# exp(k) times v by one matmul of 64 columns a head, the constant inside the queries' sum, and moved ranks in an attention and two-layer kernel

## The chip, the cores and the metric

One core of one Trainium2 chip. The metric is the device time of one execution in microseconds (us). TensorE is called PE (its weight loads PEld), VectorE DVE, ScalarE ACT, GpSimd POOL, SyncE SP. SP issues the DMAs.

## What is computed

```
k_s  = exp(k - max_s k);  k_s /= sum_s k_s + 1e-9          # per batch, head, column; q alike, along its last axis
kv   = einsum('bhsd,bhse->bhde', k_s, v)                   # 8 batches, 8 heads, 576 rows, 64 columns
x    = einsum('bhsd,bhde->bhse', q_s, kv)  -> (4608, 512)
x    = relu(x @ w_in)**2 @ w_out                           # 512 -> 2048 -> 512
out  = (sigmoid(x @ w_gate) * (x @ w_val)) @ w_out2        # 512 -> 1536 -> 512
```

The inputs of the matrices are 64-bit floats and are turned into 32-bit words on the chip.

## The kernel before

**Blocks.** The 4608 rows are nine blocks `j` of 512. Two heads stand side by side in 128 columns, so there are four pairs `p`. For each batch `b` and pair `p` (32 calls) the keys go through `k_max` (maxima on DVE, lines 430 and 434), `k_turn` and `k_all` (transpose and spreading on PE, lines 440 and 452), `k_sub` (DVE, line 457), `k_exp` (ACT, line 461), `k_mm` (PE, line 467), `k_rec` (DVE) and `k_copy` (ACT, line 479). In `k_mm`, five float32 matmuls, one for each 128 rows of the sequence, contract exp(k) of both heads (128 columns, stationary) with v of both heads and a column of ones (129 columns, moving). Of the 128x128 result only the two diagonal 64x64 blocks are used; the column at 128 holds the sums. The ones come with v from the input: its rows are 130 wide, 128 of v, a one (zero in the padding rows) and a zero.

**Queries.** For each block and pair: maxima (`q_red`), `q_sub`, `q_exp`, sums (`q_red`), `q_sum`, `q_mul`, a transpose, and `q_mm` with the batch's kv (line 577). For blocks from 2 on a row of 64 columns is split over two partition groups, and `q_swap` (PE, line 524, 16 moving columns) brings the other half's sum, which `q_both` adds; `q_sum` then adds 1e-9 and takes the reciprocal.

**The two layers.** Each large product is made of three matmuls on rounded high and low parts (`mm3`, lines 217 to 219). Blocks 0 to 2 pass `w_in` and `w_out` one by one (`conv_in`, `conv_out`); the other blocks go in pairs through seven products of 2x2 blocks. Weights are loaded raw (`plan_raw`, tile `wraw`, lines 254 to 284), split (`plan_split`, `whl`), combined (`plan_sums`, line 298), stored to DRAM and fetched again when used (`plan_fetch`, `ws`). `plan_first` and `plan_late` prepare the first layer's weights, `plan_w` those of the second (nine calls).

**Order.** Nothing is issued in the order of the loops. Every step is given to a planner by `add(rank, {engine: us}, name, function, ..., after, take, give)`. `Plan.trace` runs a list schedule on the host: for each engine it takes, among the steps whose predecessors are done in its own reckoning, the one of lowest rank, and issues it; `take` and `give` count buffers. So ranks and the assumed durations (and `LATENCY` and `slack`) set only the order in which each engine's queue is filled, SP's too; on the chip each queue runs in that order and waits by semaphores. Ranks are built from stage starts: `T0` (block 0 passes `w_in`), `T2`, `T3`, `T4`, `T1`, with the steps `TS0`, `TS1`, `TS2` of a slice of 128 columns of the first layer. `plan_k` and `plan_q` rank the steps of keys and queries at `key + n * step`; `plan_blocks` places blocks 1 to 8.

Of the kernel before, what the change touches and what calls it, by code (L numbers as in the profile page):

```python
# [29 lines left out]
class Plan:  # L30
# [3 lines left out]

    LATENCY = {DMA: 3.0, PE: 0.2, DVE: 0.13, ACT: 0.15}
    LOOK = 48
# [106 lines left out]
def attention_mlp_mlp(  # L143
# [178 lines left out]
    def plan_split(kind, g, i, b, t, ts, after, give=(), htag="W"):  # L322
        key = (kind, g, i)
        add(t, {ACT: AS}, ("wh",) + key, w_hi, key, b, htag, after=after, take=[htag])
        add(t + 0.2, LOW, ("wo",) + key, w_lo, key, b, CHOSEN, after=[("wh",) + key], give=give)
        add(ts, {DMA: 1.5}, ("ws",) + key, w_store, key, after=[("wo",) + key], slack=STORE, give=[] if htag == "X" else ["W"])

# [34 lines left out]
    def plan_first(kind, g, times, tag):  # L362

        ready, own = {}, {}
        for b in range(4) if kind == "in" else (0, 2, 1, 3):
            t = times[b]
            done = plan_raw(kind, g, b, t - 8, tag, 8.0)
            i = SPLIT[b]
            plan_split(kind, g, i, b, t - 5, t - 4, done, htag="X")
            end = [("wo", kind, g, i)]  # L370
            if kind == "in":
                add(t - 3.9, {DMA: 0.8}, ("w32", kind, g, b), w_store32, (kind, g, b), after=done)
                end.append(("w32", kind, g, b))
# [16 lines left out]
    def plan_w(kind, g, T, dT, tag):  # L390

        ready = {b: plan_raw(kind, g, b, T + b * dT, tag, 6.0) for b in range(4)}
        t = T + 4 * dT
# [25 lines left out]
    def v_load(b, p):  # L419
        vt = tile4("W", "vt", F32, (128, RK, 2 * D + 2)) if b == 0 else tile2("v", "vt", (128, RK, 2 * D + 2))  # L420
        nc.sync.dma_start(out=vt, in_=v[b, p])
        vt_t[b, p] = vt

    def k_max(b, p, r):
# [38 lines left out]
    def k_mm(b, p):  # L463
        kt, vt = kt_t.pop((b, p)), vt_t.pop((b, p))
        ps = kps[b, p]
        for r in range(RK):
            nc.tensor.matmul(ps[:, 0:2 * D + 1], kt[:, r, :], vt[:, r, 0:2 * D + 1], start=(r == 0), stop=(r == RK - 1))  # L467

    def k_rec(b, p):
        ri = sp.tile([128, 1], F32, tag="kri", name="kri")  # L470
        nc.vector.tensor_scalar(out=ri, in0=kps[b, p][:, 2 * D:2 * D + 1], scalar1=1e-9, scalar2=None, op0=ALU.add)
        nc.vector.reciprocal(out=ri, in_=ri)
        kmx[b, p] = ri

    def k_copy(b, p):
        ps, ri = kps.pop((b, p)), kmx.pop((b, p))
        for h in range(2):
            s = slice(D * h, D * h + D)
            nc.scalar.activation(out=kvf[b % 2][p][s, s], in_=ps[s, s], func=AF.Copy, scale=ri[s])

# [64 lines left out]
    def q_sum(j, p):  # L545
        sm, s2 = q_both(j, p, ALU.add)
        nc.vector.tensor_scalar(out=s2, in0=s2, scalar1=1e-9, scalar2=None, op0=ALU.add)
        nc.vector.reciprocal(out=s2, in_=s2)
# [48 lines left out]
    kv_users = defaultdict(list)  # L597
    SLACK = 2.5
    slack = lambda j: SLACK if j > 4 else 0.0

    def plan_k(b, p, key, step, wait=()):
# [20 lines left out]
    def plan_q(j, p, key, step):  # L622
# [9 lines left out]
        if not pe:  # L632
            add(key + 2.3 * step, {PE: 0.15}, ("qbw",) + n, q_swap, j, p, after=[("qb",) + n], take=["pa"], slack=slack(j))
        add(key + 2.5 * step, {DVE: 0.36 if pe else 0.55}, ("qr",) + n, q_sum, j, p, after=[("qb" if pe else "qbw",) + n], give=[] if pe else ["pa"])
        add(key + 3 * step, {DVE: TT}, ("qm",) + n, q_mul, j, p, after=[("qr",) + n], give=["qr"])
# [286 lines left out]
    T1 = T4 + TS2 * F1 + 4  # L922
# [8 lines left out]
    for g in range(NU):  # L931
        plan_late("in", g, T3 + 10 + 35 * g, 4.0, "w")

    kvs = [("kv", 0, p) for p in range(NP)]

    def conv_fetch(j, kind, g, ii, t):

        if j:
            for i in ii:
                plan_fetch((kind, g, i), c_use(j, kind, g, i), t - 14)  # L940

    def conv_in(j, f, t):
# [6 lines left out]
        for kt in range(KT):  # L949
# [11 lines left out]
            if f % 2 and kt % 2:  # L961
                add(t, {FREE: 0.0}, ("cf", j, f, kt), lambda: None, after=[("ch", j, f, kt)] + ([] if j else [("ws", "in", g, i)]), give=[tag])
        add(t + 2.6, {ACT: 1.17}, ("cg", j, f), c_g, j, f, after=[("ch", j, f, KT - 1)], take=["f"])

    def conv_out(j, f, t):
# [5 lines left out]
        if f % 2 == 0:  # L971
            conv_fetch(j, "out", g, ii, t)
        add(t - 2.5, {ACT: AS}, ("chi", j, f), c_hi, j, f, after=[("cg", j, f)], take=["S"])
        add(t - 2, LOW, ("clo", j, f), c_lo, j, f, CHOSEN, after=[("chi", j, f)], give=["f"])
# [61 lines left out]
    def plan_in(uid, t, kind, g, xn, n, tags, last_unit, slow):  # L1036
# [3 lines left out]
        def pe(i, pr, t, wait):  # L1040
            use = (uid, i)
            plan_fetch((kind, g, i), use, t - 14)
            names = []
# [21 lines left out]
    def out_seven(n, h, js, G, t):  # L1065
# [6 lines left out]
        def pe(i, pr, t, wait):  # L1072
            for kk in range(4):
                if kk % 2 == 0:
                    plan_fetch(("out", 2 * h + kk // 2, i), (uid, i, kk // 2), t - 14)
                nm = ("p", uid, i, kk)
# [8 lines left out]
        def load(nm, b, t):  # L1085
            k_ = key(nm, b)
            add(t - 14, {DMA: 0.8}, ("old",) + k_, o_ld7, k_, (uid, nm, b), after=[("ost",) + k_ + (0,), ("p", ("u1", n, 1, 1), 3, 1)], take=["a"])
            return ("old",) + k_
# [16 lines left out]
    def in_stage(n, t):  # L1105
# [3 lines left out]
        mm = MM if len(js) > 1 else MH  # L1109
        plan_x(("X1", n), js, t - 22, ("x",), nt)  # L1110
        for h in range(2):
            G = ("G", n, h)
            gready = defaultdict(dict)
            for u in range(2):
# [4 lines left out]
                for b in range(2):  # L1119
                    for nm in ("s1", "s5", "s2"):  # L1120
                        add(t - 1, {ACT: 1.17, DVE: TT}, E(nm + "g", b), e_relu2, uid, nm, b, CHOSEN, after=[end[nm][b]])
                    add(t + 0.2, {ACT: 1.17}, E("p4g", b), e_relu2p, uid, "p4", prs[0], b, nt, "f", after=[end["p4"][b]], take=["f"])
# [4 lines left out]
            for kk in range(4):  # L1127
# [4 lines left out]
                for qn, (name, where) in gready[kk].items():  # L1132
# [5 lines left out]
                    ready[qn] = [("gbind", nm, qn)]  # L1138
                times = {i: t + 24 * mm * SLOW * x + 6 * mm * kk - 6 for x, i in enumerate(PRODUCTS)}
                plan_b(nm, ready, times, "S", nt, {qn: ["f"] for qn in ready})  # L1140
# [59 lines left out]
    def gate_stage(n, t):  # L1200
# [26 lines left out]
        for kk in range(gv_n):  # L1227
# [49 lines left out]
    for stage, n in STAGES:  # L1277
# [3 lines left out]
        else:  # L1281
            x_before["gate", n] = before
            before = [("xl", "x2", j, kt) for j in GATE[n] for kt in range(KT)]
    plan_blocks([1], T0 + 6, TS0 * F1 - 20)
    plan_blocks([2], T2 + 6, TS1 * F1 - 30)
    plan_blocks(IN[0], T3 + 5, (T1 - T3 - 40) / 2)

    BESIDE = {0: 1, 1: 2}
    t = T1
    for i, (stage, n) in enumerate(STAGES):  # L1290
        if i in BESIDE:
            js = IN[BESIDE[i]]
            plan_blocks(js, t + 4, ((D1 if stage is in_stage else D2_) - 60) / len(js))
# [76 lines left out]
```

## Time and profile before

| | before |
|---|---|
| median of 3 runs | 1667.49 us (1666.01 to 1671.13) |
| the profiled execution | 1665.63 us, its span 1663.9 us |
| mean granted clock of TensorE | 0.998 |
| PE busy | 1625.4 us (98%) |
| DVE busy | 1224.7 us (74%) |
| ACT busy | 939.1 us (56%) |
| DMA | 470.50 MB, mean 283 GB/s |

The busy times are of one execution, which the hardware profiler recorded; the span goes from its first to its last instruction. Matmuls are pipelined: one is still running when the next starts, so the mean of one is longer than its share of PE's time. A float32 matmul stands in the trace as two passes, each with a weight load of its own.

### The profile page before, as it was taken

How to read it: one execution, taken by the hardware profiler on the slowest of the kernel's cores; microseconds unless marked ns; L12 is line 12 of the kernel's file. 1: busy time of each engine (PE TensorE's matmuls, PEld its weight loads, DVE VectorE, ACT ScalarE, POOL GpSimd, SP SyncE). 2: the span in 40 equal slices, each digit the busy share in tenths (PEclk: the TensorE clock that was granted, in tenths of full speed). 3: DMA queues.
4: the chain of work that ended last, by engine and by line, in shares of the span. 5: the costliest groups of instructions: out<-in, count | busy, mean ns of one | idle time of the engine just before them, and what ended most of it. 6: DMA issues, size and time to landing. Idle time of an engine off the chain costs nothing.

```text
span 1663.9 us, 24397 instructions
## 1 busy us (share of the span) xinstructions
PE 1625.4 (98%) x8644; PEld 1391.4 (84%) x8644; DVE 1224.7 (74%) x2307; ACT 939.1 (56%) x1672; POOL 2.0 (0%) x14
## 2 busy tenths in 40 slices
PE   6899999999999999999999999999999999999998
PEld 4687788877888878888878889888988899889998
DVE  8999946779999999999797486347724683448446
ACT  5876745558686776777774354335533453335344
POOL 0000000000000000000000000000000000000000
PEclk9999999999999999999999999999999999999999
DMA  7999998799799979898989667766676667665896
GB/s 278 335 365 327 346 367 333 276 333 396 268 343 327 352 261 338 287 370 317 346 329 372 232 201 233 230 196 209 223 231 195 194 204 240 197 194 178 262 376 248
DMA packets 156633, 470.50 MB, mean 283 GB/s; under 512 B 16480, under 2 KB 25696, under 8 KB 156512
## 3 DMA queue, kind: packets, MB, share of 16 engines
q1 hardware_dynamic: 156512, 468.94, 80.7%
q8 instruction: 69, 1.13, 0.3%
q14 instruction: 52, 0.43, 0.1%
HBM read 372.93 MB, written 95.94 MB: 282 GB/s over the span
## 4 chain that ended last, share of the span: by engine, by line
PE 88%; DVE 6%; ACT 3%; DMA 2%; issue 1%; SPq 0%; DVEq 0%; ACTq 0%
PE bank L217 28%; PE bank L219 28%; PE bank L218 28%; PE kps L467 2%; PE xps L577 2%; DVE bS L214 1%; DMA ws<-w_in 1%; DMA qt<-in_q_dram 1%; DVE bX L214 1%; DVE whl L214 0%; DVE xp L733 0%; PE qsw L524 0%; DVE s L671 0%; DVE wf L284 0%; DMA w_gv<-whl 0%
## 5 line engine op out<-in xcount | busy, mean ns | idle before, releaser
L217 PE MATMUL bank<-bX,ws 128*128 128x512 f32 (+1 forms) x1176 | 445.0, 378 | 2.6 <-DMA ws<-w_in 2.5
L218 PE MATMUL bank<-bX,ws 128*128 128x512 f32 (+1 forms) x1176 | 440.2, 374 | 0.0
L219 PE MATMUL bank<-bX,ws 128*128 128x512 f32 (+1 forms) x1176 | 440.1, 374 | 0.0
L733 DVE TENSOR_TENSOR s<-s,bank 128x512 f32<-128x512 f32 (+1 forms) x297 | 191.4, 654 | 216.2 <-PE bank L219 177.6
L211 ACT ACTIVATE s<-bank 128x512 f32<-128x512 f32 (+1 forms) x297 | 168.4, 572 | 213.5 <-PE bank L219 210.3
L211 ACT ACTIVATE bS<-s 128x512 fp32r<-128x512 f32 (+1 forms) x330 | 194.8, 601 | 132.0 <-PE bank L219 112.5
L214 DVE TENSOR_TENSOR bS<-s,bS 128x512 fp32r<-128x512 f32 (+1 forms) x330 | 214.5, 656 | 62.6 <-ACT bS L211 62.1
L217 PEld LDWEIGHTS bank<-bX,ws 128*128 128x128 f32 x1176 | 221.6, 188 | 42.7 <-DMA ws<-w_in 3.3
L219 PEld LDWEIGHTS bank<-bX,ws 128*128 128x128 f32 x1176 | 221.4, 188 | 40.0
L218 PEld LDWEIGHTS bank<-bX,ws 128*128 128x128 f32 x1176 | 221.7, 189 | 37.8 <-issue 0.5
L217 PE MATMUL bank<-ws,bS 128*128 128x256 f32 x756 | 214.0, 283 | 0.0
L218 PE MATMUL bank<-ws,bS 128*128 128x256 f32 x756 | 213.9, 283 | 0.0
L219 PE MATMUL bank<-ws,bS 128*128 128x256 f32 x756 | 213.9, 283 | 0.0
L752 ACT ACTIVATE s<-s 128x512 f32<-128x512 f32 (+1 forms) x120 | 70.8, 591 | 154.2 <-DVE s L733 153.9
L217 PEld LDWEIGHTS bank<-ws,bS 128*128 128x128 f32 x756 | 145.0, 192 | 1.2 <-ACT s L211 0.4
L218 PEld LDWEIGHTS bank<-ws,bS 128*128 128x128 f32 x756 | 145.1, 192 | 0.7
L219 PEld LDWEIGHTS bank<-ws,bS 128*128 128x128 f32 x756 | 145.1, 192 | 0.0
L217 PE MATMUL bank<-bS,ws 128*128 128x512 f32 x336 | 134.2, 400 | 1.3 <-issue 0.4
L218 PE MATMUL bank<-bS,ws 128*128 128x512 f32 x336 | 131.4, 391 | 1.9 <-DVE bS L214 1.9
L219 PE MATMUL bank<-bS,ws 128*128 128x512 f32 x336 | 131.1, 390 | 0.0
L671 DVE TENSOR_TENSOR s<-s,s 128x512 f32<-128x512 f32 (+1 forms) x192 | 122.2, 655 | 1.7 <-ACT s L739 0.2
L211 ACT ACTIVATE whl<-wf 128x512 fp32r<-128x512 f32 x127 | 78.8, 628 | 38.5 <-DVE wf L284 20.4
(115 smaller groups left out, 2408.1 us busy)
## 6 DMA issues: line engine op xcount, KB each, us to landing
ws<-w_out SPq DMA_DIRECT2D x221, 512.0 KB, 4.9
ws<-w_gv SPq DMA_DIRECT2D x210, 512.0 KB, 4.3
ws<-w_in SPq DMA_DIRECT2D x116, 512.0 KB, 6.4
w_out<-whl SPq DMA_DIRECT2D x53, 512.0 KB, 5.2
w_gv<-whl SPq DMA_DIRECT2D x42, 512.0 KB, 5.2
w_in<-whl SPq DMA_DIRECT2D x32, 512.0 KB, 4.8
wraw<-in_moe_w_out_dram SPq DMA_DIRECT2D x28, 512.0 KB, 6.8
vt<-in_v_dram SPq DMA_DIRECT2D x32, 325.0 KB, 6.4
```

Of the source, the lines that this page charges most:

```text
L211: nc.scalar.activation(out=dst, in_=src, func=AF.Copy)
L214: by_name[engine].tensor_tensor(out=dst, in0=src, in1=hi.bitcast(F32), op=ALU.subtract)
L217: nc.tensor.matmul(ps, ah, bh, start=first, stop=False, skip_group_check=True)
L218: nc.tensor.matmul(ps, ah, bl, start=False, stop=False, skip_group_check=True)
L219: nc.tensor.matmul(ps, al, bh, start=False, stop=last, skip_group_check=True)
L467: nc.tensor.matmul(ps[:, 0:2 * D + 1], kt[:, r, :], vt[:, r, 0:2 * D + 1], start=(r == 0), stop=(r == RK - 1))
L577: nc.tensor.matmul(ps[:, e], kvf[b % 2][p], t[:, e], start=True, stop=True)
L671: by_name[engine].tensor_tensor(out=t[o], in0=t[a], in1=t[b], op=ALU.subtract)
L733: nc.vector.tensor_tensor(out=t, in0=t, in1=banks[pr[b]][:, 0:n], op=ALU.add)
L752: nc.scalar.activation(out=t, in_=t, func=AF.Sigmoid)
```

## The change

Four things. `k_mm` makes one product a head: 64 columns of exp(k) stationary, v of that head and ones (65 columns) moving, ten matmuls a call in place of five, into partitions 0 to 63 and 64 to 127. The ones must stand beside either head's columns, so the tile of v gets two columns in front, and a new step `v_ones` on ACT copies the column of ones of each row to the place before it; `k_mm` waits for it. The sums of both heads then stand in column 64. `q_sum` puts the constant and the swapped half into one operation for blocks from 2 on. And ranks, leads and assumed durations are moved in nearly all planning functions.

```diff
-    LATENCY = {DMA: 3.0, PE: 0.2, DVE: 0.13, ACT: 0.15}
+    LATENCY = {DMA: 3.3, PE: 0.2, DVE: 0.13, ACT: 0.15}
...
-        vt = tile4("W", "vt", F32, (128, RK, 2 * D + 2)) if b == 0 else tile2("v", "vt", (128, RK, 2 * D + 2))
-        nc.sync.dma_start(out=vt, in_=v[b, p])
+        vt = tile4("W", "vt", F32, (128, 2 + RK * VC)) if b == 0 else tile2("v", "vt", (128, 2 + RK * VC))
+        nc.sync.dma_start(out=vt[:, 2:].rearrange("p (r c) -> p r c", c=VC), in_=v[b, p])
         vt_t[b, p] = vt
+
+    def v_ones(b, p):
+
+        vt = vt_t[b, p]
+        row = vt[:, 2:].rearrange("p (r c) -> p r c", c=VC)
+        pad = vt[:, 0:RK * VC].rearrange("p (r c) -> p r c", c=VC)
+        nc.scalar.activation(out=pad[:, :, 1:2], in_=row[:, :, 2 * D:2 * D + 1], func=AF.Copy)
...
         for r in range(RK):
-            nc.tensor.matmul(ps[:, 0:2 * D + 1], kt[:, r, :], vt[:, r, 0:2 * D + 1], start=(r == 0), stop=(r == RK - 1))
+            for h in range(2):
+                c = VC * r + (D + 2 if h else 1)
+                nc.tensor.matmul(
+                    ps[D * h:D * h + D, D - D * h:2 * D + 1 - D * h], kt[:, r, D * h:D * h + D], vt[:, c:c + D + 1],
+                    start=(r == 0), stop=(r == RK - 1), skip_group_check=True,
+                )
...
-            nc.scalar.activation(out=kvf[b % 2][p][s, s], in_=ps[s, s], func=AF.Copy, scale=ri[s])
+            c = slice(0, D) if h else slice(D + 1, 2 * D + 1)
+            nc.scalar.activation(out=kvf[b % 2][p][s, s], in_=ps[s, c], func=AF.Copy, scale=ri[s])
...
     def q_sum(j, p):
-        sm, s2 = q_both(j, p, ALU.add)
-        nc.vector.tensor_scalar(out=s2, in0=s2, scalar1=1e-9, scalar2=None, op0=ALU.add)
+        if j >= NPE:
+            sm = q_st[j, p]
+            s2 = sm.rearrange("p g o -> p (g o)")
+            nc.vector.scalar_tensor_tensor(
+                out=s2, in0=s2, scalar=1e-9, in1=q_ps.pop((j, p))[:, 0:N // qu_cols(j)], op0=ALU.add, op1=ALU.add
+            )
+        else:
+            sm, s2 = q_both(j, p, ALU.add)
+            nc.vector.tensor_scalar(out=s2, in0=s2, scalar1=1e-9, scalar2=None, op0=ALU.add)
         nc.vector.reciprocal(out=s2, in_=s2)
...
-    SLACK = 2.5
+    SLACK = 2.92
...
+        add(key + 2.5 * step, {ACT: 0.22}, ("vo",) + n, v_ones, b, p, after=[("vt",) + n])
...
-        add(key + 4 * step, {PE: 1.08}, ("kp",) + n, k_mm, b, p, after=[("ke",) + n, ("vt",) + n], give=big, slack=slack(b))
+        add(key + 4 * step, {PE: 0.65}, ("kp",) + n, k_mm, b, p, after=[("ke",) + n, ("vo",) + n], give=big, slack=slack(b))
...
-            done = plan_raw(kind, g, b, t - 8, tag, 8.0)
+            done = plan_raw(kind, g, b, t - 8.0, tag, 4.82)
...
-    T0, TS0, TS1 = 30.0, 4.45, 6.2
-    TS2 = 3.4
+    T0, TS0, TS1 = 25.04, 4.45, 6.19
+    TS2 = 3.72
...
     for p in range(NP):
-        plan_k(0, p, 3.0 * p, 0.6)
-        plan_q(0, p, 3.0 * p + 2, 0.6)
+        plan_k(0, p, 2.84 * p, 0.44)
+        plan_q(0, p, 2.84 * p + 1.86, 0.71)
...
                 for b in new:
-                    plan_k(b, p, t, 1.0, x_before.get(j, []))
-                plan_q(j, p, t + 2, 1.0)
+                    plan_k(b, p, t, 1.25, x_before.get(j, []))
+                plan_q(j, p, t + 2.0, 1.18)
...
-    plan_blocks([1], T0 + 6, TS0 * F1 - 20)
-    plan_blocks([2], T2 + 6, TS1 * F1 - 30)
-    plan_blocks(IN[0], T3 + 5, (T1 - T3 - 40) / 2)
+    plan_blocks([1], T0 + -1.15, TS0 * F1 - 2.23)
+    plan_blocks([2], T2 + 2.67, TS1 * F1 - 36.5)
+    plan_blocks(IN[0], T3 + 4.94, (T1 - T3 - 26.85) / 2)
...
-                plan_w(kind, g, T4 + (t + 40 - T4) / len(preps) * m, 10.0, "w")
+                plan_w(kind, g, T4 + 30.0 + (t + 110.0 - T4 - 30.0) / len(preps) * m, 10.0, "w")
```

Left out are further moved ranks of the same kind: splits (`t` to `t + 1.1`, their stores `ts` to `ts + 6.64`), fetches (`t - 14` to between `t - 14` and `t - 14.74`, one to `t - 5.03`), the steps `cg` and `chi` of the first blocks, the start of `plan_late`, and the blocks beside the later stages.

## Rows read from the trace of the kernel before

**Rows 1.** The page, busy us, share of the span, instructions:
```profile
PE 1625.4 (98%) x8644; PEld 1391.4 (84%) x8644; DVE 1224.7 (74%) x2307; ACT 939.1 (56%) x1672; POOL 2.0 (0%) x14
```

**Rows 2.** The page, the chain that ended last, by engine:
```profile
PE 88%; DVE 6%; ACT 3%; DMA 2%; issue 1%; SPq 0%; DVEq 0%; ACTq 0%
```

**Rows 3.** Busy us by stretch (A:B and its length, then the engines, clock, DMA):
```profile
0.00:20.00 20.00, 9.41 (x38) 7.21 (x38) 12.39 (x35) 7.50 (x13) 1.95 (x14) 1.00 0.82 292
20.00:120.00 100.00, 90.05 (x421) 68.81 (x422) 94.01 (x210) 83.23 (x154) 0.00 (x0) 0.98 0.92 329
120.00:200.00 80.00, 73.16 (x347) 60.33 (x346) 74.92 (x164) 53.17 (x95) 0.00 (x0) 0.98 0.95 344
200.00:340.00 140.00, 140.00 (x675) 117.01 (x674) 92.84 (x194) 76.92 (x135) 0.00 (x0) 1.00 0.88 323
...
380.00:680.00 300.00, 298.45 (x1405) 244.59 (x1405) 292.08 (x590) 223.59 (x404) 0.00 (x0) 1.00 0.90 325
...
870.00:1664.00 794.00, 789.69 (x4785) 710.25 (x4783) 458.17 (x779) 339.63 (x605) 0.00 (x0) 1.00 0.70 233
```

**Rows 4.** PE's waits, longest in total first (us, times, longest):
```profile
PE bank L440 <- DVE kmx L434: 8.8, 2, 5.7
PE kps L467 <- ACT kt L461: 6.0, 4, 2.7
```

**Rows 5.** Line 467 by stretch (PE, PEld, clock, DMA share, GB/s):
```profile
0.00:30.00 30.00, 6.98 (x40) 6.57 (x40) 1.00 0.76 272
30.00:380.00 350.00, 22.29 (x160) 20.64 (x160) 0.99 0.93 335
380.00:680.00 300.00, 15.31 (x120) 15.23 (x120) 1.00 0.90 325
```

**Rows 6.** The chain in order of time, one call of `k_mm` (start, us):
```profile
231.76 1.11 PE kps L467 x10
```

**Rows 7.** PE's timeline around that call (start, us):
```profile
231.15 0.39 PE L218 MATMUL bank<-x,ws 128*128 128x512 f32 x1
231.38 0.39 PE L219 MATMUL bank<-x,ws 128*128 128x512 f32 x1
231.60 1.27 PE L467 MATMUL kps<-vt,kt 128*128 128x129 f32 x10
...
232.95 0.40 PE L218 MATMUL bank<-x,ws 128*128 128x512 f32 x1
```

**Rows 8.** PE's timeline around one `q_swap`, line 524:
```profile
115.44 0.29 PE L524 MATMUL qsw<-qst,swap 128*128 128x16 f32 x2
...
115.89 0.40 PE L218 MATMUL bank<-g0hl,whl 128*128 128x512 f32 x1
```

**Rows 9.** Groups of instructions by line and shape (busy us, mean ns; idle before):
```profile
L467 PEld LDWEIGHTS kps<-vt,kt 128*128 128x128 f32 x280 | 35.9, 195 | 9.6 <-ACT kt L461 7.5 <-DMA vt<-in_v_dram 0.5
L479 ACT ACTIVATE kv<-kps,kri 64x64 f32<-64x64 f32 x56 | 17.3, 308 | 11.6 <-DVE kri L472 11.2
```

**Rows 10.** The tile vt: whom it waited for (us, times), and its loads:
```profile
  DMA vt<-in_v_dram: 0.5, 1
...
DMA to landing us min/median/max: 3.0/6.4/9.3
```

**Rows 11.** Groups of DVE instructions, queries' sum and preparation of weights:
```profile
L547 DVE TENSOR_SCALAR qst<-qst 128x16 f32<-128x16 f32 x28 | 4.9, 175 | 1.0
L264 DVE TENSOR_SCALAR wf<-wf 128x512 f32<-128x512 f32 x68 | 28.5, 423 | 13.9 <-ACT wf L254 13.6
L277 DVE SCALAR_TENSOR_TENSOR wf<-wraw,wf 128x512 int32<-128x512 int32 x68 | 46.5, 690 | 0.3
L214 DVE TENSOR_TENSOR whl<-wf,whl 128x512 fp32r<-128x512 f32 x127 | 86.0, 690 | 7.8 <-ACT whl L211 7.6
```

**Rows 12.** SP's timeline, two issues that follow each other (start, us):
```profile
7.36 1.12 SPq L244 DMA_DIRECT2D wraw<-in_moe_w_in_dram  x2
14.45 0.33 SPq L502 DMA_DIRECT2D qt<-in_q_dram  x1
```

More of the change, by code (lines that the diff above doesn't have):

```diff
@@ L323, in plan_split @@
         key = (kind, g, i)
-        add(t, {ACT: AS}, ("wh",) + key, w_hi, key, b, htag, after=after, take=[htag])
+        add(t + 1.1, {ACT: AS}, ("wh",) + key, w_hi, key, b, htag, after=after, take=[htag])
         add(t + 0.2, LOW, ("wo",) + key, w_lo, key, b, CHOSEN, after=[("wh",) + key], give=give)
-        add(ts, {DMA: 1.5}, ("ws",) + key, w_store, key, after=[("wo",) + key], slack=STORE, give=[] if htag == "X" else ["W"])
+        add(ts + 6.64, {DMA: 1.5}, ("ws",) + key, w_store, key, after=[("wo",) + key], slack=STORE, give=[] if htag == "X" else ["W"])
     def plan_raw(kind, g, b, t, tag, lead):
@@ L390, in plan_w @@
     def plan_w(kind, g, T, dT, tag):
-        ready = {b: plan_raw(kind, g, b, T + b * dT, tag, 6.0) for b in range(4)}
+        ready = {b: plan_raw(kind, g, b, T + b * dT, tag, 6.87) for b in range(4)}
         t = T + 4 * dT
@@ L410, in attention_mlp_mlp @@
     kps = {}
+    VC = 2 * D + 2
     KT0 = 2 * D + 128
@@ L466, in k_mm @@
         for r in range(RK):
-            nc.tensor.matmul(ps[:, 0:2 * D + 1], kt[:, r, :], vt[:, r, 0:2 * D + 1], start=(r == 0), stop=(r == RK - 1))
+            for h in range(2):
[4 more added lines that the diff above has]
+                )
     def k_rec(b, p):
         ri = sp.tile([128, 1], F32, tag="kri", name="kri")
-        nc.vector.tensor_scalar(out=ri, in0=kps[b, p][:, 2 * D:2 * D + 1], scalar1=1e-9, scalar2=None, op0=ALU.add)
+        nc.vector.tensor_scalar(out=ri, in0=kps[b, p][:, D:D + 1], scalar1=1e-9, scalar2=None, op0=ALU.add)
         nc.vector.reciprocal(out=ri, in_=ri)
@@ L633, in plan_q @@
             add(key + 2.3 * step, {PE: 0.15}, ("qbw",) + n, q_swap, j, p, after=[("qb",) + n], take=["pa"], slack=slack(j))
-        add(key + 2.5 * step, {DVE: 0.36 if pe else 0.55}, ("qr",) + n, q_sum, j, p, after=[("qb" if pe else "qbw",) + n], give=[] if pe else ["pa"])
+        add(key + 2.5 * step, {DVE: 0.36 if pe else 0.42}, ("qr",) + n, q_sum, j, p, after=[("qb" if pe else "qbw",) + n], give=[] if pe else ["pa"])
         add(key + 3 * step, {DVE: TT}, ("qm",) + n, q_mul, j, p, after=[("qr",) + n], give=["qr"])
@@ L921, in attention_mlp_mlp @@
     T4 = T3 + TS1 * F1
-    T1 = T4 + TS2 * F1 + 4
+    T1 = T4 + TS2 * F1 + 4.0
     for p in range(NP):
-        plan_k(0, p, 3.0 * p, 0.6)
-        plan_q(0, p, 3.0 * p + 2, 0.6)
+        plan_k(0, p, 2.84 * p, 0.44)
+        plan_q(0, p, 2.84 * p + 1.86, 0.71)
     for g in range(NU):
@@ L931, in attention_mlp_mlp @@
     for g in range(NU):
-        plan_late("in", g, T3 + 10 + 35 * g, 4.0, "w")
+        plan_late("in", g, T3 + 15.32 + 35.0 * g, 4.0, "w")
     kvs = [("kv", 0, p) for p in range(NP)]
@@ L939, in conv_fetch @@
             for i in ii:
-                plan_fetch((kind, g, i), c_use(j, kind, g, i), t - 14)
+                plan_fetch((kind, g, i), c_use(j, kind, g, i), t - 14.74)
     def conv_in(j, f, t):
@@ L962, in conv_in @@
                 add(t, {FREE: 0.0}, ("cf", j, f, kt), lambda: None, after=[("ch", j, f, kt)] + ([] if j else [("ws", "in", g, i)]), give=[tag])
-        add(t + 2.6, {ACT: 1.17}, ("cg", j, f), c_g, j, f, after=[("ch", j, f, KT - 1)], take=["f"])
+        add(t + 1.63, {ACT: 1.17}, ("cg", j, f), c_g, j, f, after=[("ch", j, f, KT - 1)], take=["f"])
     def conv_out(j, f, t):
@@ L972, in conv_out @@
             conv_fetch(j, "out", g, ii, t)
-        add(t - 2.5, {ACT: AS}, ("chi", j, f), c_hi, j, f, after=[("cg", j, f)], take=["S"])
+        add(t - -3.85, {ACT: AS}, ("chi", j, f), c_hi, j, f, after=[("cg", j, f)], take=["S"])
         add(t - 2, LOW, ("clo", j, f), c_lo, j, f, CHOSEN, after=[("chi", j, f)], give=["f"])
@@ L1041, in pe @@
             use = (uid, i)
-            plan_fetch((kind, g, i), use, t - 14)
+            plan_fetch((kind, g, i), use, t - 14.55)
             names = []
@@ L1074, in pe @@
                 if kk % 2 == 0:
-                    plan_fetch(("out", 2 * h + kk // 2, i), (uid, i, kk // 2), t - 14)
+                    plan_fetch(("out", 2 * h + kk // 2, i), (uid, i, kk // 2), t - 5.03)
                 nm = ("p", uid, i, kk)
@@ L1086, in load @@
             k_ = key(nm, b)
-            add(t - 14, {DMA: 0.8}, ("old",) + k_, o_ld7, k_, (uid, nm, b), after=[("ost",) + k_ + (0,), ("p", ("u1", n, 1, 1), 3, 1)], take=["a"])
+            add(t - 10.36, {DMA: 0.8}, ("old",) + k_, o_ld7, k_, (uid, nm, b), after=[("ost",) + k_ + (0,), ("p", ("u1", n, 1, 1), 3, 1)], take=["a"])
             return ("old",) + k_
@@ L1109, in in_stage @@
         mm = MM if len(js) > 1 else MH
-        plan_x(("X1", n), js, t - 22, ("x",), nt)
+        plan_x(("X1", n), js, t - 22.0, ("x",), nt)
         for h in range(2):
@@ L1120, in in_stage @@
                     for nm in ("s1", "s5", "s2"):
-                        add(t - 1, {ACT: 1.17, DVE: TT}, E(nm + "g", b), e_relu2, uid, nm, b, CHOSEN, after=[end[nm][b]])
+                        add(t - 1.12, {ACT: 1.17, DVE: TT}, E(nm + "g", b), e_relu2, uid, nm, b, CHOSEN, after=[end[nm][b]])
                     add(t + 0.2, {ACT: 1.17}, E("p4g", b), e_relu2p, uid, "p4", prs[0], b, nt, "f", after=[end["p4"][b]], take=["f"])
@@ L1138, in in_stage @@
                     ready[qn] = [("gbind", nm, qn)]
-                times = {i: t + 24 * mm * SLOW * x + 6 * mm * kk - 6 for x, i in enumerate(PRODUCTS)}
+                times = {i: t + 24 * mm * SLOW * x + 6 * mm * kk - 6.85 for x, i in enumerate(PRODUCTS)}
                 plan_b(nm, ready, times, "S", nt, {qn: ["f"] for qn in ready})
@@ L1206, in gate_stage @@
             for kt in range(KT):
-                add(t - 40, {DMA: 0.8}, ("xl", "x2", j, kt), x2_load, j, kt, after=[("ost", j, kt, 1)] + x_before["gate", n], take=["x"])
+                add(t - 40.0, {DMA: 0.8}, ("xl", "x2", j, kt), x2_load, j, kt, after=[("ost", j, kt, 1)] + x_before["gate", n], take=["x"])
         xn = ("X2", n)
-        plan_x(xn, js, t - 24, ("xl", "x2"), nt)
+        plan_x(xn, js, t - 22.12, ("xl", "x2"), nt)
         Y = ("Y", n)
@@ L1241, in gate_stage @@
             add(t - 6 + kk, {FREE: 0.0}, ("bind", nm), bind, after=[("e", x[0], x[4], x[2]) for x in blocks.values()])
-            times = {i: t + per * x + 1.42 * kk - 6 for x, i in enumerate(PRODUCTS)}
+            times = {i: t + per * x + 1.42 * kk - 6.0 for x, i in enumerate(PRODUCTS)}
             plan_b(nm, {qn: [("bind", nm)] for qn in blocks}, times, "S", nt, {qn: [x[3]] for qn, x in blocks.items()})
@@ L1251, in pe @@
                 if kk % 2 == 0:
-                    plan_fetch(("out2", kk // 2, i), use, t - 14)
+                    plan_fetch(("out2", kk // 2, i), use, t - 14.0)
                 nm = ("p", uid, i, kk)
@@ L1292, in attention_mlp_mlp @@
             js = IN[BESIDE[i]]
-            plan_blocks(js, t + 4, ((D1 if stage is in_stage else D2_) - 60) / len(js))
+            plan_blocks(js, t + -5.78, ((D1 if stage is in_stage else D2_) - 60.03) / len(js))
         if stage is gate_stage and n == 0:
```

## The prediction
> **What bounds the kernel now.** I read the busy shares first. PE is at 98% of the span, DVE at 74%, ACT at 56% [rows 1], and the chain that ended last is 88% PE [rows 2]. A busy PE alone proves little, so next come the stretches [rows 3]. From 200 to 340 us PE is busy in every us, from 380 to 680 us in 298.45 of 300, from 870 us to the end in 789.69 of 794. What PE leaves empty lies at the start: 20.00 − 9.41 = 10.6 us in the first 20, 9.95 in the next 100, 6.8 in 120 to 200. Two kinds of gain are therefore open: less PE work inside the full stretches, worth its own time; and fewer waits before 200 us.
>
> Second reading: DVE is nearly as full as PE in two of these stretches, 94.01 of 100 us (20 to 120) and 292.08 of 300 (380 to 680) [rows 3]. PE time removed there counts only while DVE keeps up. The list of waits [rows 4] says who ended PE's idle time: DVE's maxima of the first keys (8.8 us), the exponentials in front of `k_mm` (6.0 us in 4 waits), and nothing else comes to as much: the rest is a sum of small waits.
>
> **The matmul of exp(k) and v.** There are 32 calls of `k_mm`, 28 of them after 30 us ([rows 5]: 40 passes in the first 30 us, 160 to 380 us, 120 after). A call is five float32 matmuls, which the trace shows as ten passes of 129 columns. The chain gives such a call 1.11 us, a pass 0.111 us [rows 6]. The timeline agrees: from the first pass at 231.60 to the second of the following matmuls at 232.95 are 1.35 us, of which one 0.23 us pitch belongs to the wide matmul between, so 1.12 [rows 7].
>
> After the change a call is ten matmuls, twenty passes of 65 columns with 64 stationary columns each, two heads into different halves of the partitions. No row of before has 64 stationary columns, so I bound a pass. By its streamed columns: 0.111 × 65/129 = 0.056 us. But a pass of `q_swap` streams only 16 columns and does not get cheaper: from 115.44 to 115.89 lie two of them and one wide matmul, (0.45 − 0.23)/2 = 0.11 us [rows 8]. So the 128 stationary columns alone can hold a pass to 0.11 us, and if 64 of them held it as long, a call would be 20 × 0.111 = 2.22 us. If the load shrinks with its columns, it is 20 × 0.056 = 1.12 us with the passes one after the other, and 0.56 us with the two heads side by side, as they write different partitions from different stationary columns. Then there are edges. A 512-column matmul lasts 0.39 us while its successor starts 0.23 us behind it [rows 7]: 0.16 us of overlap, which is lost at each end of a call if PE first runs empty, 0.56 + 0.32 = 0.88 us. I take 0.72, side by side with half of the edge cost, since the rows bound both ends and decide neither. Ends: 0.56 and 2.22.
>
> The gain is 28 × (1.11 − 0.72) = 10.9 us in stretches where PE is what is full. The four calls of the first 30 us lie where PE waits anyway; I count 0 for them.
>
> Here a rule speaks against the change. The Trainium skill, TensorEngine Tiling (Array Packing), section Tiling Modes, says that changing the tiling mode drains the engine; by it the call would be the 0.88 us of both full edges, the sum 28 × 0.23 = 6.4 us, and no run so far shows such a change of mode. The same page (section Overview) gives up to a factor of 2 for at most 64 columns; by that alone the call would be 0.56 us and the gain 15.4 us.
>
> **What is added for it.** `v_ones`, one ACT operation of 128x5 elements in each of the 32 calls. The smallest ACT group of the trace is the 64x64 copy at 308 ns [rows 9]; no cheaper one is shown, so it lies between 0 and 0.31 us, in all at most 10 us on an engine busy 223.59 of 300 us in the fullest long stretch [rows 3]. Off the path I count 0. In the first 30 us four of them stand in a chain that alternates between DVE, ACT and PE: 4 × 0.31 = 1.2 at most, and I take +0.6. It also adds a wait: the copy needs `vt`, and behind it on ACT stand `k_exp` and evictions. A `vt` load lands after 3.0 / 6.4 / 9.3 us (least, median, most), and in before the matmul waited only once, for 0.5 us, for it [rows 10]. The copy ranks 1.5 steps ahead of the matmul, so it needs `vt` some 1 to 2 us sooner; the cover is that lead, and without it ACT stands.
>
> **Queries' sum.** For 28 of 36 blocks an add and a constant add of 175 ns become one operation. At full width scalar_tensor_tensor and tensor_tensor take the same 0.69 us, so I price the joined one as the add alone; saved are 28 × 0.175 = 4.9 us of DVE [rows 11]. PE does not wait for it where PE is full: 0 for the time. Its worth is cover: with 12 calls (120 passes) in 380 to 680 us PE sheds 12 × 0.39 = 4.7 us there, and DVE has only 7.9 us free in the 300 that it shares.
>
> **Preparation of the last weights.** Nine calls of `plan_w` are ranked from 30 us later and spread to 70 us further. One is DVE work of 4 × (2 × 0.42 + 2 × 0.69) on the raw blocks, 7 × 0.69 for the low parts and 4 × 0.69 for the sums, 16.5 us, all nine 148 us (the two steps at 0.42 and the four at 0.69 have one row each, [rows 11]). Some of it leaves the full stretch for that after 870 us, where DVE is busy 458.17 of 794 [rows 3]. I count 0: it keeps DVE from becoming the next bound there. Uncovered, the fetches of the gate weights would come late; I allow 3 us for that in the range.
>
> **Ranks at the start.** The ranks order instructions and set no times, so what counts is which DMA or operation passes which. The first-matrix work moves 5 us ahead of the rest, the steps of the first blocks are closer, block 1 starts about 12 us sooner in rank and spreads over the whole stage. DVE is idle 20.00 − 12.39 = 7.6 us in the first 20 and then almost full for 100 [rows 3]; any operation put into those 7.6 us takes its time off the end of that stage. SP is what holds it: after 8.5 us the next load leaves at 14.45, a `qt` waiting for its buffer with the third `wraw` behind it [rows 12]. With the weight loads' ranks moved (the first from 30 − 16 = 14 to 25.04 − 12.86 = 12.2) some of them pass this one. I take half of the 7.6 us: −3.8. The 6.0 us of waits on exponentials [rows 4] could shrink with the longer steps of blocks 1 and 2, but every rank moves and new waits of 1 to 3 us are as likely to appear: 0, with 5 us each way in the range.
>
> **The sum.** −10.9 + 0.6 − 3.8 = −14.1 on the profiled execution's 1665.63 us (span 1663.9 and 1.7 around it): 1651.5. The median of the runs shown is 1.9 above the profiled one, so I say 1653.
>
> **Rivals.**
> A. Edges cost in full, or more if the first load of a call also cannot run ahead (up to 0.19 us each [rows 9], which ends at 1.26 us, slightly dearer than now). In full: −6.4 − 3.2 = −9.6, 1656 and with the offset 1658. For: the 0.16 us overlap exists in every row pair. Against: passes of 16, 129 and 512 columns follow each other now without any loss beyond their pitch [rows 7, 8].
> B. The heads do not run side by side: 1.12 us a call, no gain on PE, −3.2 from the start alone: 1662, with the offset 1664. For: today's passes come at a fixed pitch one after the other, and no row shows two at once. Against: nothing in the rows either.
> C. Slower: a load of 64 columns holds a pass as long as one of 128. Place: every call; price 28 × 1.11 = +31 us; about 1694, with the offset 1696. For: the 16-column passes. It decides as soon as a pass holds PE over 0.07 us one after another (28 × (20 × 0.07 − 1.11) = 8 us, more than the start gives back). Against: load and stream are nearly equal at 128 columns, which is what a price per column gives on both sides. The Trainium skill, TensorE: Matmul & The Clock Gate, section LDWEIGHTS, has the load go by its columns; that would exclude C, and the rows, all of 128 columns, cannot show it.
> D. The new order loses: `v_ones` or a moved load stands at the head of ACT or SP and holds what is behind it. A `vt` 2 us late in ten of the 28 calls is 20 us of ACT, more than the 14.1: about 1672. Against: the single wait of 0.5 us.
>
> **Chances.** Forecast 0.60 (its own range 1643 to 1660), A 0.19, B 0.10, C 0.04, D 0.07. A difference below about 0.3%, 5 us, cannot be told from none. The forecast and A lie beyond it but for 0.03 (0.585 + 0.175 faster); B splits 0.04 faster, 0.05 same, 0.01 slower; C is slower; D 0.02 same, 0.05 slower. That is 0.80 / 0.10 / 0.10. The range 1641 to 1665 leaves out C, D, half of B and thin tails of the rest, below 0.2. Its low end is the 0.56 us call (−15.4) with the 7.6 us of the start and some of the waits.
>
> **What would show it.** The chain's piece for `k_mm` at about 0.6 us instead of 1.11 (over 1.0: B; 2 or more: C); the gap to the wide matmul before and after it at 0.16 beyond its pitch (A). DVE's busy time in the first 20 us at 14 or more. No wait of ACT's `v_ones` for `vt` over 1 us. PE still full from 380 to 680 us: if it starts to wait for DVE there, the removed PE time was not the bound. The prediction is wrong if the twenty passes take as long as the ten.

## The result, and the profile after

The changed kernel takes 1645.78 us in the median of four runs (1644.65 to 1647.69), the kernel before, run beside it, 1666.75. The ratio is 0.9871 (95% interval 0.985 to 0.9892): 21 us or 1.3% less, half as much again as the 14 us that were forecast. The profiled execution took 1644.98 us with a span of 1643.2, 20.7 less than that of before.

The page of after, busy times and then the chain by engine:

```profile
PE 1614.1 (98%) x8964; PEld 1374.7 (84%) x8964; DVE 1221.5 (74%) x2278; ACT 942.2 (57%) x1707; POOL 1.9 (0%) x14
...
PE 94%; DVE 3%; ACT 1%; DMA 1%; issue 1%; SPq 0%; ACTq 0%
```

PE's part of the chain rose from 88 to 94% [rows 2]. That share does not say what went; the busy times do: PE's work fell by 11.3 us (1625.4 to 1614.1, [rows 1]) and its empty time by 9.4 (38.5 to 29.1). The stretches of after (PE, PEld, DVE, ACT, POOL; granted clock, DMA share, GB/s):

```profile
0.00:20.00 20.00, 10.39 (x60) 6.87 (x61) 14.16 (x36) 9.44 (x20) 1.87 (x14) 1.00 0.81 299
20.00:120.00 100.00, 88.56 (x494) 65.33 (x493) 94.81 (x213) 83.19 (x158) 0.00 (x0) 0.98 0.91 334
120.00:200.00 80.00, 75.95 (x409) 61.15 (x409) 76.84 (x162) 57.31 (x106) 0.00 (x0) 1.00 0.97 357
200.00:340.00 140.00, 140.00 (x752) 115.47 (x751) 87.91 (x181) 72.91 (x134) 0.00 (x0) 1.00 0.94 339
340.00:380.00 40.00, 40.00 (x200) 32.80 (x198) 39.03 (x79) 28.52 (x53) 0.00 (x0) 1.00 0.96 342
380.00:680.00 300.00, 299.78 (x1526) 243.11 (x1526) 289.03 (x559) 225.24 (x414) 0.00 (x0) 1.00 0.88 314
```

The one of these stretches that [rows 3] leave out was, in before:

```profile
340.00:380.00 40.00, 36.40 (x159) 29.13 (x158) 28.47 (x53) 22.29 (x38) 0.00 (x0) 1.00 0.96 349
```

Beside these rows: PE's empty time in 120 to 200 us went from 6.8 to 4.1, in 340 to 380 from 3.6 to nothing, in 380 to 680 from 1.5 to 0.2; in the first 120 us nothing was won (20.5 before, 21.1 now). The starts of the n-th wide matmul (lines 217 to 219) of both traces, set side by side, show where the 20.2 us of the last one came from:

```
n-th wide matmul   0    192   288   480   960   1200  1600  2400  3000  3500  last
before (us)       32.8  97.8 122.4 181.7 312.5 373.0 485.1 691.6 828.0 944.4 1659.4
after - before    -0.9  -1.2  -0.3  -5.6 -10.3  -9.4 -11.6 -17.7 -17.7 -20.2  -20.2
```

Of the 5.3 us between 122 and 182 us, 1.7 are the clock's: in before it was at 1.2 GHz for 3.4 us from 131 us on (0.98 in that stretch), in after it stayed at 2.4 (1.00).

A call of `k_mm` now, in the chain (start, us) and in PE's timeline around it:

```profile
230.25 0.73 PE kps L477 x20
```

```profile
229.64 0.39 PE L218 MATMUL bank<-x,ws 128*128 128x512 f32 x1
229.86 0.39 PE L219 MATMUL bank<-x,ws 128*128 128x512 f32 x1
230.18 0.80 PE L477 MATMUL kps<-vt,kt 128*64 128x65 f32 x20
230.91 0.50 PE L217 MATMUL bank<-x,ws 128*128 128x512 f32 x1
231.25 0.39 PE L218 MATMUL bank<-x,ws 128*128 128x512 f32 x1
```

Read as before [rows 7]: without the call the matmul at 231.25 would start two pitches of 0.23 behind the one at 229.86, so the call costs 1.39 − 0.46 = 0.93 us. By the same reading the call of before costs 231.38 to 232.95 less two pitches, 1.11. The twenty passes alone span 0.80, of which the last one's length of 0.22 belongs to the pipeline: 0.58 us for nineteen starts, 0.61 for twenty. The other 0.32 us are the two edges: the first pass starts 0.32 behind its predecessor in place of 0.23, and the remaining 0.23 are lost behind the last. A call of before has no such edges: its 1.11 us are ten passes of 0.111.

### The profile page after: what moved, and what is told of

Read it like the earlier page. It is cut to its first block, busy times and chain, and to the rows that moved or that the text cites. A ratio compares the mean times of both kernels' runs of the same rounds, so it can differ in the third digit from the quotient of the medians.

```text
span 1643.2 us, 25041 instructions
## 1 busy us (share of the span) xinstructions
PE 1614.1 (98%) x8964; PEld 1374.7 (84%) x8964; DVE 1221.5 (74%) x2278; ACT 942.2 (57%) x1707; POOL 1.9 (0%) x14
## 4 chain that ended last, share of the span: by engine, by line
PE 94%; DVE 3%; ACT 1%; DMA 1%; issue 1%; SPq 0%; ACTq 0%
PE bank L217 30%; PE bank L218 30%; PE bank L219 30%; PE xps L598 2%; PE kps L477 1%; PE qsw L538 0%; DMA ws<-w_in 0%; DVE wf L277 0%; DMA wraw<-in_moe_w_in_dram 0%; DVE qst L528 0%; DVE whl L214 0%; PE kps L460 0%; DVE wf L284 0%; DMA qt<-in_q_dram 0%; ACT g L838 0%
```

## The experiments

Each was timed in alternation with the kernel before; a ratio is against that, with its 95% interval. Differences to the changed kernel are of medians, to 1645.8. They are rougher than the ratios: the kernel before had medians of 1668.0 us beside e1 to e4, 1668.6 beside e5 to e7, 1666.1 beside e8 to e11 and 1666.9 beside e12, against 1666.75 beside the changed kernel.

**e1, the wide matmul in the new order.** v_ones is still issued.

```diff
-            for h in range(2):
-                c = VC * r + (D + 2 if h else 1)
-                nc.tensor.matmul(ps[D * h:D * h + D, D - D * h:2 * D + 1 - D * h], kt[:, r, D * h:D * h + D], vt[:, c:c + D + 1], ...)
+            nc.tensor.matmul(ps[:, 0:2 * D + 1], kt[:, r, :], vt[:, 2 + VC * r:2 + VC * r + 2 * D + 1], ...)
...                       # the sums are read in column 128 again
```

> The changed kernel with the five matmuls of 129 columns put back (ones column of v as it was read, sums in column 128); v_ones still issued, every queue in the same order. Theory: in the trace of after a call and its edges cost 0.93 us against 1.12, so 28 calls x 0.19 = 5.3 us are lost: 1651. Rival (the new order was made for short calls and hides nothing longer): all of 28 x 0.46 = 13 us or more, 1659. Rival (the matmul was worth nothing): 1646.

Measured: 1651.46 us, 5.7 more; ratio 0.9911 (0.989 to 0.9932). The matmul is worth what its calls show in the trace, and the rest of the change, in the main the moved ranks, the other 0.9%, about 15 us.

**e2, the new matmul in the old order.**

```diff
+        if (b, p) in vt_t:      # behind the exponential; else ahead of the matmul
+            v_ones(b, p)
...
+            for h in range(2):  # as in the change
```

> The kernel before with the matmuls of 64 columns a head alone; the copy of the ones stands behind the exponential on ACT (or just ahead of the matmul where v is not yet asked for), every other instruction of every queue in the order of before. Theory: 28 x 0.19 = 5.3 us less than before, 1661.5. If the matmul explains all of the result: 1646. If only together with the new order: 1667.

Measured: 1660.09 us, ratio 0.9962 (0.9948 to 0.9975), 6.3 us less by the ratio. It works without the new order, for the same 5 to 6 us.

**e3, head after head.**

```diff
-        for r in range(RK):
-            for h in range(2):
+        for h, r in [(h, r) for h in range(2) for r in range(RK)]:
...                       # the body as in the change
```

> The changed kernel with the ten matmuls of a call ordered head after head (five into partitions 0 to 63, then five into 64 to 127) in place of alternating. Theory (neighbours run at the same time only when they write different halves): twenty passes at 0.058 one after another, 1.16 in place of 0.58 us, 28 x 0.58 = +16 us, 1662. Rival (the short pass comes from the smaller load alone, not from two at once): unchanged, 1646.

Measured: 1658.32 us, 12.5 more; ratio 0.9941 (0.9924 to 0.9959). PE's timeline around one call of this kernel:

```profile
200.84 1.20 PE L476 MATMUL kps<-vt,kt 128*64 128x65 f32 x20
...
201.97 0.50 PE L217 MATMUL bank<-x,ws 128*128 128x512 f32 x1
202.31 0.40 PE L218 MATMUL bank<-x,ws 128*128 128x512 f32 x1
```

The same twenty passes span 1.20 in place of 0.80 us. The single passes do halve with their columns (0.058 us against 0.111), but there are twice as many. So the short call of after comes from two passes running at once when neighbours write different halves of the partitions, not from the smaller load alone. The price is 0.40 us a call, 28 × 0.40 = 11.2, and not the expected 0.58: the starts in the trace stand 0.058 apart, but around the change of head three pairs start together.

**e4, the old queries' sum.**

```diff
+        sm, s2 = q_both(j, p, ALU.add)
+        nc.vector.tensor_scalar(out=s2, in0=s2, scalar1=1e-9, scalar2=None, op0=ALU.add)
...                       # for all blocks, in place of both branches of the change
```

> The changed kernel with the queries' sum of before (two DVE operations in place of one, 28 times), PE, ACT and SP in the same order. Theory: DVE has room, 1646 to 1647. Rival (DVE bounds 380 to 680 us): up to 28 x 0.175 = +4.9 us, 1651.

Measured: 1646.69 us, 0.9 more and inside the spread of the runs; ratio 0.987 (0.9852 to 0.9889). The joined operation is worth nothing here, although it does cost only one add (0.166 us in the median, as the add of before).

**e5, the last weights' preparation as before.**

```diff
-                plan_w(kind, g, T4 + 30.0 + (t + 110.0 - T4 - 30.0) / len(preps) * m, 10.0, "w")
+                plan_w(kind, g, T4 + (t + 40 - T4) / len(preps) * m, 10.0, "w")
```

> The changed kernel with the ranks of the last weights' preparation (plan_w) of before. Theory: the later preparation is what freed PE between 340 and 700 us, where the changed kernel gained 8 us, of which the matmul explains 2: +4 to +6 us, 1650 to 1652. Rival (it does not matter, DVE keeps up): 1646.

Measured: 1665.78 us, 20 more; ratio 0.9988 (0.9977 to 1.0). Far more than expected. PE's waits of this kernel from 335 to 400 us (us, times, longest), where after has none:

```profile
PE kps L448 <- DVE kmx L442: 2.4, 1, 2.4
PE kps L477 <- ACT kt L469: 1.7, 1, 1.7
PE xps L598 <- DVE qtr L579: 1.5, 1, 1.5
PE bank L217 <- DMA ws<-w_out: 1.4, 1, 1.4
```

So 5.6 of these 7.0 us are waits for the keys' and queries' operations on DVE and ACT, and 1.4 for a transfer. From 336 to 367 us the granted clock was at 1.2 GHz for 13.7 us in all (two stretches of the trace); PE was busy in 10.8 of them, which costs, by an estimate, half of that, 5.4 us. A part of the profiled loss is not the edit's: at 202 us, where the queues are still those of after, the profiled execution is already 5.5 us behind. How much of the 20 belongs to the preparation itself and how much to ranks that no longer fit each other, this run does not say. The next gives what the same ranks are worth in the old order.

**e8, the same ranks alone in the kernel before.** The diff is that of the change in this line.

> The kernel before with the moved ranks of the last weights' preparation alone. Theory (the later preparation takes DVE work and transfers out of 330 to 700 us): the waits of 340 to 380 us (3.6) and some after go, 4 to 8 us less than before, 1660 to 1664. Rival (these ranks only fit the other moved ranks, as undoing them cost 20 us there): within 3 us of before, or slower.

Measured: 1658.21 us, ratio 0.9953 (0.9938 to 0.9969), 7.8 us less by the ratio. The stretch from 340 to 400 us, of before, of e8 and of e5:

```profile
340.00:400.00 60.00, 56.28 (x256) 45.45 (x255) 47.07 (x92) 37.95 (x67) 0.00 (x0) 1.00 0.98 369
```

```profile
340.00:400.00 60.00, 60.00 (x283) 49.97 (x282) 50.04 (x100) 39.90 (x71) 0.00 (x0) 1.00 0.98 356
```

```profile
340.00:400.00 60.00, 56.20 (x250) 45.51 (x250) 50.14 (x95) 39.71 (x72) 0.00 (x0) 0.91 0.95 357
```

PE's 3.7 us of waiting go; over all of 335 to 1640 us PE's empty time falls from 6.9 to 1.3 us, which is most of the 7.8. Whom PE waited for there, in before:

```profile
PE bank L217 <- DMA ws<-w_in: 2.5, 2, 2.1
PE bank L217 <- DMA ws<-w_out: 1.1, 1, 1.1
```

These are transfers. Two things made them late. First, SP's queue, from which they are issued one after the other:

```profile
344.68 0.41 SPq L307 DMA_DIRECT2D ws<-w_out  x1
352.42 0.32 SPq L302 DMA_DIRECT2D w_gv<-whl  x1
352.83 0.38 SPq L307 DMA_DIRECT2D ws<-w_out  x1
353.27 1.28 SPq L307 DMA_DIRECT2D ws<-w_in  x2
```

SP's waits for the split that comes ahead of a store, from 340 to 370 us (us, times, longest), in before

```profile
SPq L302 <- DVE whl L214: 12.0, 3, 7.2
```

and in e8

```profile
SPq L302 <- DVE whl L214: 1.1, 1, 1.1
```

In before the store of a prepared weight (`w_gv`, line 302) stood at the head of SP's queue for 7.2 us, until DVE had split that weight, and the two loads behind it left at 352.83 and 353.27, landed at 357.19 and 359.17 and ended PE's waits at 357.23 and 359.21 (1.1 and 0.3 us). Second, the transfers themselves, whose engines were 98% busy from 340 to 400 us: the load that ended the longest wait (2.1 us) was issued at 370.65 and took 7.3 us. The medians of those issued between 340 and 380 us, in before:

```profile
ws<-w_in SPq DMA_DIRECT2D x11, 512.0 KB, 8.3
w_gv<-whl SPq DMA_DIRECT2D x7, 512.0 KB, 7.5
```

and of e8:

```profile
ws<-w_in SPq DMA_DIRECT2D x12, 512.0 KB, 5.1
w_gv<-whl SPq DMA_DIRECT2D x5, 512.0 KB, 6.0
```

There are fewer stores beside them, but the share of the transfers is the same 98% in e8, so how much of the shorter landing is due to the stores is not shown. So the step that was to keep DVE free took waits for weight loads off the path, and it did so by way of DVE as well: the store that held SP's queue waited for DVE.

**e10 and e11, that preparation 10 us earlier and 10 us later in rank.**

```diff
-  T4 + 30.0 + (t + 110.0 - T4 - 30.0)
+  T4 + 20.0 + (t + 100.0 - T4 - 20.0)     # e10; e11: 40.0 and 120.0
```

> The changed kernel with the ranks of the last weights' preparation 10 us earlier than it has them. If the amount of work moved decides, a sixth to a third of what undoing it cost, 1647 to 1652, on the way from 1646 to 1666. If the order that happens to come out decides, anything from 1645 to 1666, with no relation to the 10 us.

> The changed kernel with the ranks of the last weights' preparation 10 us later than it has them. If the amount of work moved decides: 1643 to 1647. If the order that happens to come out decides: anything up to 1666.

Measured: 1649.80 (ratio 0.9905, 0.9882 to 0.9928) and 1655.07 us (0.9929, 0.9903 to 0.9955). Both are slower in the medians, though e10's interval overlaps that of the change (0.985 to 0.9892). Earlier is within what was expected, but in the profiled executions more than half of it is not for the expected reason: of the 4.4 us that e10 is behind after at the end, it has lost 2.4 by 202 us, where the queues of the two kernels are the same (they are up to 308 us), and 2.0 after that. The stretch 155 to 165 us of after and of e10:

```profile
155.00:165.00 10.00, 8.24 (x55) 6.76 (x55) 9.90 (x22) 6.89 (x13) 0.00 (x0) 1.00 1.02 387
```

```profile
155.00:165.00 10.00, 8.32 (x50) 6.41 (x49) 8.58 (x19) 6.68 (x13) 0.00 (x0) 0.83 1.01 376
```

Behind the same wait of PE for an exponential, 1.8 us in the one and 1.7 in the other, the clock stayed at 2.4 GHz in after and fell to 1.2 for 3.4 us in e10, which costs 1.7 us of PE work. By 202 us, with equal queues, e5 and e11 too are 5.5 and 4.8 us behind after; the clock was at 1.2 GHz for 10.2 us up to there in e10 and e11 and for 17.1 in e5, against 3.4 in after. Later has a cause of its own besides: from 959 us on PE waits for evictions on ACT, in whose queue late weights (`whl`) are split,

```profile
PE bank L217 <- ACT s L211: 3.8, 2, 2.0
```

```profile
960.29 0.61 ACT L211 ACTIVATE whl<-wf 128x512 fp32r<-128x512 f32 x1
960.81 0.58 ACT L211 ACTIVATE s<-bank 128x512 f32<-128x512 f32 x1
```

and from 962.5 us on the clock is at 1.2 GHz for 6.8 us. Between 924 and 1003 us e11 falls back by 6.6 us. The prediction allowed 3 us for late fetches of the gate weights; this wait is another one, and the change stays clear of it by less than 10 us of rank.

**e6 and e9, the start: put back in the changed kernel, and alone in the kernel before.**

```diff
-    T0, TS0, TS1 = 25.04, 4.45, 6.19
+    T0, TS0, TS1 = 30.0, 4.45, 6.2
-        plan_k(0, p, 2.84 * p, 0.44)
+        plan_k(0, p, 3.0 * p, 0.6)
-    plan_blocks([1], T0 + -1.15, TS0 * F1 - 2.23)
+    plan_blocks([1], T0 + 6, TS0 * F1 - 20)
...                       # e6; with plan_q(0, ...) and the raw loads' lead; e9 is the reverse
```

> The changed kernel with the starting ranks of before (T0 30, block 0 at 3.0 and steps 0.6, block 1 at T0 + 6, raw loads 8 ahead). Theory: by 122 us the changed kernel had gained 0.3 us in all, so the start is worth nothing there, 1645 to 1648. Rival (what the start brings is paid out at 122 to 270 us, where 8 us were gained): +4 to +7 us, 1650 to 1653.

> The kernel before with the moved starting ranks alone (T0, block 0's places and steps, block 1's place, the lead of the raw loads). Theory (DVE's empty time in the first 20 us is filled and paid out by 270 us): 4 to 7 us less, 1661 to 1664. Rival (only with the other ranks): within 3 us of before, or slower.

Measured: e6 1652.33 us, 6.5 more than after (ratio 0.99, 0.988 to 0.992); e9 1666.56, ratio 1.0007 (0.9992 to 1.0021), nothing. The start is worth nothing by itself. What e6 lost is in good part the clock: its five runs had a mean granted clock of 0.9946, the four of after 0.9972, and 0.0026 of 1650 us is 4.3 us (an estimate that takes PE as busy throughout).

**e7, the steps of later blocks as before.**

```diff
-                    plan_k(b, p, t, 1.25, x_before.get(j, []))
-                plan_q(j, p, t + 2.0, 1.18)
+                    plan_k(b, p, t, 1.0, x_before.get(j, []))
+                plan_q(j, p, t + 2, 1.0)
...                       # and SLACK 2.5, LATENCY of DMA 3.0
```

> The changed kernel with the steps of later blocks (1.0 and 1.0 for 1.25 and 1.18), SLACK 2.5 and the assumed DMA latency 3.0 of before. Theory: the waits of PE on exponentials between 120 and 200 us come back, 5.4 us against 1.8: +3 to +5 us, 1649 to 1651. Rival (single ranks shuffle the waits and move the sum either way): within 3 us of 1646.

Measured: 1650.60 us, 4.8 more; ratio 0.9897 (0.9881 to 0.9912). That is the theory's size, but not its cause: the waits on exponentials did not come back. PE's waits between 120 and 200 us begin with

```profile
PE kps L460 <- DVE km L454: 2.8, 2, 1.6
PE qsw L538 <- DVE qst L528: 1.5, 1, 1.5
```

and come to 4.7 us, against 4.1 in after. The clock was at 1.2 GHz for 13.7 us before 200 us, against 3.4 in after. The rival, that single ranks shuffle the waits, fits the trace better, and the ratio's interval overlaps that of the change, so it is not excluded.

**e12, start and steps together in the kernel before.** The diffs of e9 and the reverse of e7, with block 2 at `T2 + 2.67` and `TS1 * F1 - 36.5`.

> The kernel before with the moved ranks of the first 300 us together: start, block 0, block 1 and 2, the raw loads' lead, the steps of later blocks, SLACK and the assumed DMA latency. All moved ranks came to about 15 us (e1), the last weights' preparation alone to 8, the start alone to none. Theory (start and steps only work together): 5 to 8 us less than before, 1659 to 1661. Rival (what is left comes from the moved ranks of splits, stores and fetches, or from all together): within 3 us of before.

Measured: 1662.75 us, ratio 0.996 (0.9948 to 0.9973), 6.7 us less by the ratio (4.5 to 8.7) and 4.2 by the medians. Together they are worth something, alone the start is not. Where it is won the trace cannot show: the profiled execution, 1667.60 us, is the slowest of the eleven.

**Put together.** The matmul alone 0.9962, the preparation alone 0.9953, start and steps 0.9960: the product is 0.9876, and the change as a whole 0.9871. So three parts of 6 to 8 us each are enough for the result, and the moved ranks outside these groups need not bring anything; they were not tried alone. Taken back one at a time in the changed kernel, the parts cost 5.7, 20, 6.5 and 4.8 us, 37 in all. The matmul costs what it brought; the preparation costs two and a half times as much, and start and steps, with waits and the clock in the sum, 11.3 against 6.7.

## Why the prediction was right

The time (1653 forecast, 1646 measured) lies in the range and the direction was right. Step by step the sum was not: one term was half as large, and two that were set to little or nothing made it up. That the sum came within 7 us is in part luck.

**The matmul, −10.9 forecast, −5.3 by the trace, −5.7 (e1) and −6.3 (e2) on the clock.** What failed is the choice "I take 0.72": a call costs 0.93 us. Side by side was right (e3), 0.61 us; the edges are not half but all of the 0.32 us that the overlap of two wide matmuls gave. That is rival A's price, 0.88, with its passes a little slower. Only the sum agrees with it: 0.09 us are lost in front of the call and 0.23 behind it, not 0.16 at each end, so that the loss is just this overlap is not shown. The Trainium skill, TensorEngine Tiling (Array Packing), section Tiling Modes, says that a change of the tiling mode drains the engine. The trace agrees in that the call loses 0.32 us where passes of 128x64 stand between passes of 128x128, and the call of before, 128x128 throughout, none. The rows had the size of an edge; halving it for want of evidence was the mistake. In the chain the call takes 0.73 us, between the 0.6 that was to show it and the 1.0 of rival B. Rival B fell with e3, rival C with the passes at half of 0.11 us: 64 stationary columns do not hold a pass as long as 128.

**Cover of the removed PE time.** PE stays full from 380 to 680 us, 299.78 of 300, with DVE at 289.03. DVE did not become the bound, as forecast; its 4.9 us from the queries' sum were not needed for that (e4).

**The last weights' preparation, 0 forecast, −7.8 alone (e8).** The step that failed: it was priced as DVE work alone, whose relief PE would not feel. The waits of 340 to 380 us (3.6 us of empty PE) do not stand in the prediction, and they are transfers, held in SP's queue by this step's stores, which wait for DVE, and long in landing. Those waits would have named it: [rows 4] stops at the two largest, and [rows 3] leave this stretch out. In the changed kernel (e5) most of the waits that come back are on DVE and ACT themselves.

**The start, −3.8 forecast, 0 alone (e9), −6.7 with the steps (e12).** DVE's busy time in the first 20 us did rise from 12.39 to 14.16, over the 14 that was to show it, and yet PE had 0.3 us by 122 us. The sign does not tell the new start from the old one: e8, whose queues are those of before up to 308 us, has 15.24, and e9 and e12, with the new start, 13.09 and 12.28.

```profile
0.00:20.00 20.00, 8.91 (x41) 6.71 (x41) 15.24 (x38) 9.36 (x17) 1.87 (x14) 1.00 0.85 303
```

The step that failed is that the time put into DVE's gap comes off the end of that stage. In the stage DVE is at 94 to 95% either way; in the changed kernel 10 us appear between 122 and 312 us, a part of them the matmul's and the clock's, and by e9 and e12 the start brings its part only with the longer steps of blocks 1 and 2. Which instruction carries it from the one to the other was not tried, and the cause stays open. In the first weight load's rank the prediction writes 12.86 where the change gives 12.82; the 12.2 is right. SP's queue did change as said: the third raw load leaves at 12.89 us, not behind the `qt` at 14.45 [rows 12]:

```profile
11.56 0.33 SPq L516 DMA_DIRECT2D qt<-in_q_dram  x1
11.93 0.43 SPq L417 DMA_DIRECT2D kt<-in_k_dram  x1
12.41 0.43 SPq L422 DMA_DIRECT2D vt<-in_v_dram  x1
12.89 0.43 SPq L244 DMA_DIRECT2D wraw<-in_moe_w_in_dram  x1
```

The waits on the exponentials, set to 0, fell from 6.0 to 3.4 us, most of it between 120 and 200 us (5.4 to 1.8):

```profile
PE bank L448 <- DVE kmx L442: 9.0, 3, 5.4
PE kps L477 <- ACT kt L469: 3.4, 2, 1.8
```

**`v_ones`, +0.6.** One costs 0.20 us, inside the bounds of 0 and 0.31. ACT waited for `vt` through it 4.0 us in six waits, the longest 1.4, and PE for it 1.0 us once:

```profile
L430 ACT ACTIVATE vt<-vt 128x5 f32<-128x5 f32 x32 | 6.4, 201 | 4.0 <-DMA vt<-in_v_dram 4.0
```

```profile
ACT vt L430 <- DMA vt<-in_v_dram: 4.0, 6, 1.4
```

That is more than the 1 us named as the limit, and far from the 20 us of rival D. The term itself was not measured apart.

## What to carry to other kernels

A matmul of which only the two diagonal blocks are used can be split into two of half the columns, which run at once if neighbours alternate between the halves of the partitions. Each run of such passes pays at its two ends: here 0.32 us against 0.50 won in the passes, so longer runs should win more (not tried). Price moved preparation by its transfers as well as by its engine, where the loads of the main work are on the path: a store that waits for an engine holds every load behind it in the same queue. Measure moved ranks both alone and taken back: for the preparation the two differ by a factor of two and a half. And choose a sign that the kernel before does not show on its own.

## What the runs showed of the hardware

Twenty passes of 65 columns with 64 stationary columns start in pairs 0.007 us apart, a pair every 0.058 us (0.107 behind the first pair); head after head they stand singly, 0.058 apart, except around the change of head, where three pairs start together although the program has them one after the other. Behind nearly equal waits at the same place (1.8 and 1.7 us), with equal queues up to there, PE's clock fell to 1.2 GHz for 3.4 us in one kernel and not in another. By 202 us the profiled executions of kernels with equal queues lie 2.4 to 5.5 us behind after (e10, e11, e5), so an experiment on a 0.3% effect must look at the granted clock before it is believed.
